# Decay attention followed by an expert layer: the weight conversion of a block split over two steps of the job loop

## The chip, the cores and the metric

The program runs on one core of one Trainium2 chip. Its engines are TensorE (PE in the profile, with its weight loads as PEld), VectorE (DVE), ScalarE (ACT), GpSimd (POOL) and SyncE (SP, which only issues DMAs here). Each engine works through its own list of instructions in order and waits on semaphores for the others. The metric is the device time in microseconds of one execution; lower is better.

## The reference

Decay attention over 8 batches x 8 heads x 576 tokens x 64 dimensions, and then a two-layer expert network on the 4608 tokens, 512 wide inside and out and 2048 wide between:

```python
scores = (q @ k.T) / sqrt(D) + (cum[:, None] - cum[None, :])   # cum = cumsum(log f), causal
attn = softmax(scores);  x = attn @ v                            # heads side by side: 4608 x 512
h = x @ w_in                                                    # 512 x 2048
g = where(h >= 1, h, where(h <= -1, 0, (h + 1) ** 2 / 4))
out = g @ w_out                                                 # 2048 x 512
```

The two weight matrices arrive as 64-bit floats; everything else is 32-bit.

## The kernel before, in words

**Jobs.** Attention is done in jobs, one for a pair of heads of a batch (`jobs`, L80). Batch 0 is cut in two by rows: jobs 0 to 3 take row blocks 0 and 1 (128 rows each) of the four head pairs, jobs 4 to 7 row blocks 2, 3 and 4. From job 8 on, a job has all five row blocks, the last of 64 rows. Jobs 8 to 11 are batch 1, jobs 12 to 15 batch 2, and so on.

**Steps.** A job is a list of steps, one for each row block, with one more step put in for the values product of the job before (`finish`, L796): 3 steps in jobs 1 to 3, 4 in jobs 4 to 7, 6 from job 8 on. A row step (L773) computes the scores of the next row block on PE (L482), builds their decay term on POOL (L488, L492), and for its own row block takes the row minimum on DVE (L571), the exponential on ACT (L575), and writes the result in two half-precision parts, the high one on ACT (L589) and the rest on DVE (L595). These are transposed by a DMA (L601) or, in jobs 0 to 4, by matmuls on PE (`turn_rows`, L513). The last row step of job p also measures the norms of q and k of job p + 2 (`measure`, L391), and the first lines of job p prepare q and k of job p + 1 (`prepare`, L409: L414 on ACT and L416 on DVE write the tile `qs`, and a DMA, L421, transposes it). Jobs below 12 (`NQK`) don't use `qs` for this; job 12 is the first that does.

**Expert units.** A unit is a block of 256 tokens, `ch`, with a block of 256 of the 2048 columns, `fb`. Its front (`moe_front`) is 24 matmuls at L657 into a tile `ph` (48 where the tokens lie in two batches), then ACT and DVE from L666 to L671, which give the two parts of `g`. Its back (`moe_back`) is 12 matmuls at L685 into `po`. Units are handed out by quota after the steps from job 5 on, as their tokens become ready. The order of the first sixteen, written as (ch, fb), is (0,0) to (0,5), (1,0) to (1,5), (0,6), (0,7), (1,6), (1,7). In jobs 9 and 10 these are (1,0), (1,1), (1,2), one each behind steps 1, 3 and 5 of job 9, and (1,3), (1,4), (1,5) behind steps 1, 3 and 5 of job 10; job 11 takes (0,6) and (0,7), behind steps 2 and 5.

**Weight conversion.** There are 16 pieces of weights, numbered n; even ones are from w_in and odd ones from w_out, and pieces 2i and 2i + 1 make block i. `weight_load` (L201) fetches a raw piece of 1 MB to a place given by `RAW`; several pieces use the same place one after the other, so that piece 14 is fetched when piece 12 is done, and piece 15 when piece 14 is done, all three in the place called early. `weight_split` then does, for one block (a single piece for the last two):

- bits and squares: three DVE passes per piece (L211, L214, L217) turn the 64-bit words into 32-bit floats, with the scratch `bits`, which lies in the same memory as `qs`; then ACT squares them and adds them up (L221). The square's own output goes to the low half of `place[n]`, where the converted weights will stand, and that memory can be part of an earlier piece's raw place: that of piece 2 lies in the raw place of piece 0.
- norm product: a matmul of the sums with a matrix of ones on PE (L131), into a tile of the name `ph`, the one that the fronts, `turn_rows` and `across` use also. There are two such buffers.
- scales: four small DVE operations (L132 to L140).
- halves: the high part on ACT (L225), and the low part on POOL for an even piece (L227, L228) or on DVE for an odd one (L230).

`CONVERT` says how many blocks a job converts; they come behind its steps in equal parts, and ahead of the units handed out behind the same step. When the last block of a group of units is done, `moe_scales` computes the scales of that group's units (`early_z`).

**Who sets the order.** A planner at build time orders each engine's list, by the order in which the program traces the instructions and by when it reckons them ready. A few instructions are held by `in_order`: they go behind everything that their engine was given before them. L131 is one of them, and L211 another. In the profile, work of one job is often done while later jobs are running.

Of the kernel before, what the change touches and what calls it, by code (L numbers as in the profile page):

```python
# [45 lines left out]
def kernel(  # L46
# [80 lines left out]
    def from_norms(scale, power, squares):  # L127

        n = squares.shape[1]
        pt = ps.tile([P, 2, TC], F32, name="ph").rearrange("p f t -> p (f t)")  # L130
        in_order(nc.tensor.matmul(pt[:, 0:n], lhsT=ones, rhs=squares, start=True, stop=True))  # L131
        nc.vector.tensor_scalar(  # L132
            out=power, in0=pt[:, 0:n], scalar1=LOW * LOW, scalar2=HIGH * HIGH, op0=ALU.max, op1=ALU.min
        )
        nc.vector.tensor_scalar(
            out=power.bitcast(I32), in0=power.bitcast(I32), scalar1=1, scalar2=EVEN_EXP,
            op0=ALU.logical_shift_right, op1=ALU.bitwise_and,
        )
        nc.vector.tensor_scalar(out=power, in0=power, scalar1=ROOT, scalar2=None, op0=ALU.mult)
        nc.vector.reciprocal(scale, power)  # L140
# [46 lines left out]
    def raw(n):  # L187
        where = RAW[n]
        if where == "early":
            return early.bitcast(I32)[:, 0:4 * DM]  # L190
        if where == "next":
            return x1.bitcast(I32)[:, 0:4 * DM]
        return place[:, where:where + 2].rearrange("p n l c -> p (n l c)").bitcast(I32)
# [6 lines left out]
            src = w_out.bitcast(I32)[i * 2 * P:(i + 1) * 2 * P, :].rearrange("(t p) c -> p t c", p=P)  # L200
        nc.sync.dma_start(raw(n).rearrange("p (t c) -> p t c", t=src.shape[1]), src)  # L201

    def weight_split(n0, n1):
        i, j0 = divmod(n0, 2)
        both = n1 - n0
        m2 = tiny.tile([P, 2], F32, name="m2w", bufs=2)
        words = []
        for n in range(n0, n1):
            top = raw(n)[:, 1::2]
            low = raw(n)[:, 0::2]  # L210
            in_order(nc.vector.tensor_scalar(  # L211
                out=bits, in0=top, scalar1=0x07FFFFFF, scalar2=3, op0=ALU.bitwise_and, op1=ALU.logical_shift_left
            ))
            nc.vector.scalar_tensor_tensor(  # L214
                out=bits, in0=low, scalar=29, in1=bits, op0=ALU.logical_shift_right, op1=ALU.bitwise_or
            )
            nc.vector.scalar_tensor_tensor(  # L217
                out=top, in0=top, scalar=-0x40000000, in1=bits, op0=ALU.bitwise_and, op1=ALU.bitwise_or
            )
            words.append(top.bitcast(F32))  # L220
            nc.scalar.activation(place[:, n, 1], words[-1], AF.Square, accum_out=m2[:, n - n0:n - n0 + 1])  # L221
        from_norms(sw[:, j0:j0 + both, i], mp[:, j0:j0 + both, i], m2[:, 0:both])
        for n, word in zip(range(n0, n1), words):
            hi, lo, s = place[:, n, 0], place[:, n, 1], sw[:, n % 2, i:i + 1]
            nc.scalar.activation(hi, word, AF.Copy, scale=s)  # L225
            if n % 2 == 0:
                nc.gpsimd.tensor_scalar(out=word, in0=word, scalar1=s, scalar2=0.0, op0=ALU.mult, op1=ALU.add)  # L227
                nc.gpsimd.tensor_tensor(out=lo, in0=word, in1=hi, op=ALU.subtract)  # L228
            else:
                nc.vector.scalar_tensor_tensor(  # L230
                    out=lo, in0=word, scalar=s, in1=hi, op0=ALU.mult, op1=ALU.subtract
                )
# [27 lines left out]
    def value_step(b, i):  # L260

        if 0 < i <= NPAIR:
            value_max(b, i - 1)
        if i < NPAIR:
            value_load(b, i)

    def value_scale(b):
        m1 = tiny.tile([P, 1], F32, name="m1", bufs=2)
        nc.vector.tensor_reduce(out=m1, in_=vmax[b], axis=AX.X, op=ALU.max)
        m = mv[:, b:b + 1]  # L270
        across(m, m1)
        if b:
            nc.vector.tensor_tensor(out=m, in0=m, in1=mv[:, b - 1:b], op=ALU.max)
        scale_of(sv[:, b:b + 1], pv[:, b:b + 1], m)
# [84 lines left out]
    def load_decay(w, h):  # L359
        bh = w.b * H + 2 * w.hp + h  # L360
        ck = two.tile([P, S], F32, name="ck", bufs=3)
        nc.sync.dma_start(
            ck[:, 0:w.s1], cum_d[bh:bh + 1, 0:w.s1].broadcast_to([P, w.s1])
        )
        w.ck.append(ck)
# [43 lines left out]
    def prepare(w):  # L409
        if w.p < NQK:  # L410
            return early_prepare(w)
        sc = w.sc
        for j in range(2):
            nc.scalar.activation(qs[:, 2 * j], w.x32[j], AF.Copy, scale=sc[:, j:j + 1])  # L414
        for j in range(2):
            nc.vector.scalar_tensor_tensor(  # L416
                out=qs[:, 2 * j + 1], in0=w.x32[j], scalar=sc[:, j:j + 1], in1=qs[:, 2 * j],
                op0=ALU.mult, op1=ALU.subtract,
            )
        qkT = two.tile([P, 4, SP], F16, name="qkT")  # L420
        nc.sync.dma_start_transpose(  # L421
            qkT.rearrange("p c (b e) -> p (c b) e", e=P), qs.rearrange("p c e -> p (c e)")
        )
        qh, ql, kh, kl = (qkT[:, c] for c in range(4))
        w.terms = ((qh, kh), (ql, kh), (qh, kl))
# [295 lines left out]
    nw = 0  # L721
# [7 lines left out]
    def load_weights(n):  # L729
        nonlocal nload  # L730
        while nload < min(n, 2 * NB) and RAW[nload] not in RAW[nw:nload]:
            weight_load(nload)
            nload += 1

    def weight_step():
        nonlocal nw
        n = nw + (2 if nw < 2 * NB - 2 else 1)
        load_weights(n)
        weight_split(nw, n)
        nw = n  # L740
        load_weights(nw + AHEAD)
        for first, end in groups:
            if nw == 2 * end:
                z = moe_scales(0, first, end - 1, True)
                for ch, e0, e1 in EARLY:
                    if (e0, e1) == (first, end):
                        for fb in range(first, end):
                            bsc[(ch, fb)] = z
# [12 lines left out]
    for p in range(njobs + 1):  # L761
        w = pairs[p] if p < njobs else None
        nxt = pairs[p + 1] if p + 1 < njobs else None
        steps = []
        if w:
            if w.b not in xs:
                xs[w.b] = xpool.tile([P, NPAIR, 2, S], F16, name="x")
            if nxt:
                load_decay(nxt, 0)
                prepare(nxt)  # L770
            scores(w, w.r0)

            def step(r):  # L773
                if r + 1 < w.r1:
                    scores(w, r + 1)
                if r == w.r1 - 2 and nxt:
                    load_decay(nxt, 1)
                    split_values(nxt)
                weights(w, r)
                if r == w.r0 and p + 3 < njobs:  # L780
                    pairs.append(load(p + 3))
                if w.r1 == NT5 and w.b + 1 < B:
                    n = w.r1 - w.r0
                    i = w.hp * n + r - w.r0 - (NPAIR - 1) * n + -(-(NPAIR + 1) // n) * n
                    if 0 <= i <= NPAIR:
                        value_step(w.b + 1, i)
                    if w.hp == NPAIR - 1 and r == w.r0:
                        value_scale(w.b + 1)
                if r == w.r1 - 1 and p + 2 < njobs:
                    measure(pairs[p + 2])  # L790

            steps = [lambda r=r: step(r) for r in range(w.r0, w.r1)]
        if p > 0:
            wp = pairs[p - 1]

            def finish():  # L796
                nonlocal tokens
                (early_values if wp.p < NPE else values)(wp, xs[wp.b])
                if wp.hp == NPAIR - 1:
                    if wp.b and wp.r0 == 0:  # L800
                        join_scales(wp.b - 1)
                    tokens = wp.b * S + wp.s1

            steps.insert(4 if len(steps) == NT5 else 2, finish)
        load_weights(LOADS.get(p, 0))
        blocks = CONVERT.get(p, 0)
        quota = -(-ready() // (NPAIR - (p + NPAIR - 1) % NPAIR))
        before, converted = done, 0
        for i, st in enumerate(steps):
            st()  # L810
            while converted < blocks * (i + 1) // len(steps):
                weight_step()
                converted += 1
            while ready() and done - before < quota * (i + 1) // len(steps):
                if units[done] not in bsc and nw < 2 * NB:
                    break
                moe_unit(*units[done])
                done += 1
# [35 lines left out]
```

## Time and profile before

| what | time or share |
|---|---|
| median of 3 runs | 1116.96 us (1116.5 to 1118.39) |
| the profiled execution | 1118.56 us, its span 1116.8 us |
| mean granted TensorE clock | 0.966 |
| VectorE, ScalarE, GpSimd busy | 799.0, 790.0, 427.4 us |
| DMA | 152.18 MB, mean 136 GB/s |

The profiled execution is one run of its own; what lies outside its span is 1.76 us. In the views that follow, a row of the timeline has the start in microseconds, the busy time, the engine, the line, the operation and its tiles, how often it was merged, and in brackets how long the engine stood idle before it and who ended that wait. A row of the waits has the total, the number and the longest. A row of the windows has, after the stretch and its length, the busy time of PE, PEld, DVE, ACT and POOL with the number of instructions, the granted clock, the share of the DMA engines, and GB/s.

### The profile page before, as it was taken

What the parts mean: (1) busy time and instruction counts of PE and PEld (TensorE: products, weight loads), DVE (VectorE), ACT (ScalarE), POOL (GpSimd) and SP (SyncE); (2) the same over time, 40 slices, a digit from 0 to 9 for tenths busy, and PEclk for the clock granted to TensorE, in tenths of its full rate; (3) what the DMA queues carried; (4) which work ended last, traced back from release to release, by engine and by line L of the source; (5) the groups of instructions that cost most, each with busy time, mean ns of one, the idle gap of its engine ahead of it and who ended that gap; (6) DMA issues with size and microseconds to landing.
All of it is one profiled execution on the core that took longest, in us unless ns stands there. A gap on an engine that the chain in (4) does not pass through costs nothing. (4 is left out here: it accounts for less than half of the span.)

```text
span 1116.8 us, 24410 instructions
## 1 busy us (share of the span) xinstructions
PE 1017.8 (91%) x8811; PEld 663.8 (59%) x8811; DVE 799.0 (72%) x2095; ACT 790.0 (71%) x1638; POOL 427.4 (38%) x679
## 2 busy tenths in 40 slices
PE   4647789667999999999999999999999999999998
PEld 3424455335566666666766666566666666677665
DVE  4785987887989888887667668888888787322222
ACT  3665887756877887788667768787878887444443
POOL 3486665634544543343223324344343442000000
PEclk9968889778999999999999999999999999999999
DMA  7957765575978657766653666775776462200000
GB/s 235 303 143 222 167 147 125 142 191 116 190 172 166 159 143 170 167 152 148 118 140 78 155 119 153 168 174 139 166 167 155 116 124 73 66 21 1 19 20 19
DMA packets 408281, 152.18 MB, mean 136 GB/s; under 512 B 383968, under 2 KB 384992, under 8 KB 408160
## 3 DMA queue, kind: packets, MB, share of 16 engines
q1 hardware_dynamic: 408160, 150.63, 57.6%
q8 instruction: 69, 1.13, 0.4%
q14 instruction: 52, 0.43, 0.1%
HBM read 75.64 MB, written 9.58 MB: 76 GB/s over the span
## 5 line engine op out<-in xcount | busy, mean ns | idle before, releaser
L657 PE MATMUL ph<-x,place 128*128 128x256 f16 (+3 forms) x4608 | 413.3, 248 | 6.4 <-DVE u L668 5.5
L685 PE MATMUL po<-place,g 128*128 128x512 f16 x1728 | 401.9, 382 | 12.4 <-ACT g L670 8.2
L657 PEld LDWEIGHTS <-place 128*128 128x128 f16 x4608 | 354.1, 99 | 66.3 <-issue 18.0
L685 PEld LDWEIGHTS <-g 128*128 128x128 f16 x1728 | 166.4, 99 | 192.0 <-ACT g L670 10.5
L488 POOL TENSOR_SCALAR sdr<-ck,nsig,cqs 128x128 f32<-128x128 f32 (+1 forms) x192 | 145.8, 763 | 149.2 <-DVE pr L595 137.3
L575 ACT ACTIVATE sdr<-sdr,nm 128x384 f32<-128x384 f32 (+1 forms) x248 | 137.4, 554 | 66.9 <-DVE nm L571 57.0
L668 DVE SCALAR_TENSOR_TENSOR u<-ph,z,u 128x512 f32<-128x512 f32 x128 | 95.8, 748 | 113.1 <-ACT u L667 112.5
L488 POOL TENSOR_SCALAR sd<-ck,nsig,cqs 64x576 f32<-64x576 f32 x48 | 60.0, 1250 | 248.7 <-ACT qs L414 109.3
L666 ACT ACTIVATE u<-ph,z 128x512 f32<-128x512 f32 x128 | 97.9, 765 | 78.4 <-PE ph L657 78.4
L482 PE MATMUL s<-qkT 64*64 64x512 f16 (+11 forms) x1056 | 119.6, 342 | 34.1 <-DVE nm L571 30.6
L595 DVE SCALAR_TENSOR_TENSOR pr<-sdr,rc,pr 128x384 f16<-128x384 f32 (+2 forms) x232 | 130.5, 596 | 21.6 <-ACT pr L589 20.4
L670 ACT ACTIVATE g<-u,z 128x512 f16<-128x512 f32 x128 | 91.9, 718 | 67.6 <-DVE u L668 67.3
L671 DVE SCALAR_TENSOR_TENSOR g<-u,z,g 128x512 f16<-128x512 f32 x128 | 96.7, 756 | 47.2 <-ACT g L670 46.5
L589 ACT ACTIVATE pr<-sdr,rc 128x384 f16<-128x384 f32 (+1 forms) x236 | 119.3, 556 | 12.1 <-DVE rc L586 5.3
L571 DVE CUSTOM_DVE_ANT_0 sdr<-s,sdr,nalpha 128x128 f32<-128x128 f32 (+1 forms) x192 | 99.0, 545 | 13.1 <-PE s L482 8.3
L492 POOL TENSOR_SCALAR_AFFINE_SELECT sdr<-sdr 128x128 f32<-128x128 f32 x248 | 93.9, 389 | 9.7
L667 ACT ACTIVATE u<-u 128x512 f32<-128x512 f32 x144 | 89.5, 622 | 2.0
L615 PE MATMUL s<-pT,vs 128*64 128x320 f16 (+3 forms) x1098 | 70.9, 282 | 4.7 <-DVE nm L571 4.7
L615 PEld LDWEIGHTS <-vs 128*64 128x64 f16 x1098 | 49.7, 112 | 27.3 <-issue 8.8
L488 POOL TENSOR_SCALAR sdr<-ck,cq 128x384 f32<-128x384 f32 (+3 forms) x56 | 39.9, 712 | 66.2 <-DVE pr L595 38.3
L482 PEld LDWEIGHTS <-qkT 64*128 64x128 f16 (+1 forms) x864 | 33.8, 99 | 51.3 <-issue 35.9
L414 ACT ACTIVATE qs<-qk,sc 128x640 f16<-128x640 f32 x48 | 37.0, 818 | 22.4 <-DVE sc L140 22.4
(154 smaller groups left out, 1013.8 us busy)
## 6 DMA issues: line engine op xcount, KB each, us to landing
ck<-cum_d SPq DMA_DIRECT2D x64, 288.0 KB, 3.8
out_dram<-ot SPq DMA_DIRECT2D x36, 256.0 KB, 2.1
qk<-in_k_dram SPq DMA_DIRECT2D x64, 128.0 KB, 2.7
vst<-in_v_dram SPq DMA_DIRECT2D x28, 288.0 KB, 3.3
v<-in_v_dram SPq DMA_DIRECT2D x62, 128.0 KB, 2.6
qk<-in_q_dram SPq DMA_DIRECT2D x56, 128.0 KB, 2.7
place<-in_moe_w_in_dram SPq DMA_DIRECT2D x6, 1024.0 KB, 7.2
place<-in_moe_w_out_dram SPq DMA_DIRECT2D x5, 1024.0 KB, 7.2
```

The lines of the kernel that those rows point to most:

```text
L482: nc.tensor.matmul(sds[h % len(sds)][1][p0:p1, c0:c1], lhsT=a[rows, q0 - w.s0:q0 - w.s0 + p1 - p0], rhs=b[rows, c0:c1], start=(i == 0), st ...
L488: nc.gpsimd.tensor_scalar(out=sd[p0:p1, 0:wid], in0=w.ck[h][p0:p1, 0:wid], scalar1=w.nsig if w.p < NQK else w.nsig[p0:p1], scalar2=w.cqs[p ...
L571: nc.vector.tensor_tensor_reduce(out=a, in0=sp[:, 0:wid], in1=a, scale=w.nalpha, scalar=BIG, op0=ALU.add, op1=ALU.min, accum_out=nm[:, i:i ...
L575: nc.scalar.activation(a, a, AF.Exp, bias=nm[:, i:i + 1], scale=-1.0, accum_out=sm[:, i:i + 1])
L589: nc.scalar.activation(pr[:, :, 0, i, :], a, AF.Copy, scale=rc[:, i:i + 1])
L595: nc.vector.scalar_tensor_tensor(out=pr[:, :, 1, i, :], in0=a, scalar=rc[:, i:i + 1], in1=pr[:, :, 0, i, :], op0=ALU.mult, op1=ALU.subtract,)
L615: nc.tensor.matmul(av[64 * h:64 * h + 64, at + s0:at + s1], lhsT=w.vs[:, vl, h, t, :], rhs=w.pT[:, t, pl, h, s0:s1], start=(t == 0 and pi ...
L657: nc.tensor.matmul(ph[:, fi, a0:a1], lhsT=wi[fb][:, wl, t, fi * P:(fi + 1) * P], rhs=xs[b][:, t, xl, s0:s0 + a1 - a0], start=(fi == 0 and ...
L666: nc.scalar.activation(u, h, AF.Relu, scale=z.u[:, i:i + 1], bias=z.h[:, i:i + 1])
L668: nc.vector.scalar_tensor_tensor(out=u, in0=h, scalar=z.t[:, i:i + 1], in1=u, op0=ALU.max, op1=ALU.min)
L671: nc.vector.scalar_tensor_tensor(out=g[:, 1], in0=u, scalar=z.r[:, i:i + 1], in1=g[:, 0], op0=ALU.mult, op1=ALU.subtract)
L685: nc.tensor.matmul(po[ch][i], lhsT=g[:, gl, fi * TC + i * P:fi * TC + (i + 1) * P], rhs=wo[fb][:, wl, fi, :], start=(first and fi == 0 and ...
```

## The change

`weight_split` is cut in two. `weight_words` does the bits and squares of a block, `weight_halves` the norm product, scales and halves. `weight_begin`, at the place where `weight_step` stood, calls the first; `weight_end` calls the second, right behind the following step, ahead of what else stands there. `nw`, the count of pieces done, moves on in `weight_end`, and with it the loads that it allows and the call of `moe_scales`.

```diff
-    def weight_split(n0, n1):
-        i, j0 = divmod(n0, 2)
-        both = n1 - n0
+    def weight_words(n0, n1):
         m2 = tiny.tile([P, 2], F32, name="m2w", bufs=2)
         words = []
         for n in range(n0, n1):
...
             nc.scalar.activation(place[:, n, 1], words[-1], AF.Square, accum_out=m2[:, n - n0:n - n0 + 1])
+        return n0, n1, words, m2
+
+    def weight_halves(n0, n1, words, m2):
+        i, j0 = divmod(n0, 2)
+        both = n1 - n0
         from_norms(sw[:, j0:j0 + both, i], mp[:, j0:j0 + both, i], m2[:, 0:both])
...
-    def weight_step():
-        nonlocal nw
+    half = []
+
+    def weight_begin():
         n = nw + (2 if nw < 2 * NB - 2 else 1)
         load_weights(n)
-        weight_split(nw, n)
-        nw = n
+        half.append(weight_words(nw, n))
+
+    def weight_end():
+        nonlocal nw
+        if not half:
+            return
+        weight_halves(*half[0])
+        nw = half.pop()[1]
         load_weights(nw + AHEAD)
...
             st()
+            weight_end()
             while converted < blocks * (i + 1) // len(steps):
-                weight_step()
+                weight_end()
+                weight_begin()
                 converted += 1
```

By the program's text, with steps counted from 0, this is where the parts stand. The bits and squares stay where they were.

| pieces | bits and squares, and before also the rest | norm product, scales and halves now |
|---|---|---|
| 0, 1 | job 1, step 2 | job 2, step 0 |
| 2, 3 | job 2, step 2 | job 3, step 0 |
| 4, 5 | job 3, step 1 | job 3, step 2 |
| 6, 7 | job 3, step 2 | job 4, step 0 |
| 8, 9 | job 5, step 3 | job 6, step 0 |
| 10, 11 | job 6, step 3 | job 7, step 0 |
| 12, 13 | job 9, step 5 | job 10, step 0 |
| 14 | job 10, step 2 | job 10, step 3 |
| 15 | job 10, step 5 | job 11, step 0 |

The units handed out behind the step of the left column, which stood behind the norm product, now stand ahead of it: (0,1), (0,3), (1,2) and (1,5) among them.

## The prediction

> **What bounds the kernel now.** I read the busy shares first, then PE by stretches, then who PE waited for, and last the order on PE around the norm products.
>
> ```profile
> span 1116.8 us, 24410 instructions
> PE 1017.8 (91%) x8811; PEld 663.8 (59%) x8811; DVE 799.0 (72%) x2095; ACT 790.0 (71%) x1638; POOL 427.4 (38%) x679
> ```
> ```profile
> sum 164.00, PE 120.14 PEld 70.05 DVE 136.22 ACT 115.52 POOL 89.02; mean PE 15.02 PEld 8.76 DVE 17.03 ACT 14.44 POOL 11.13
> 240.00:264.00 24.00, 10.23 (x61) 5.90 (x59) 19.32 (x59) 11.45 (x18) 11.73 (x14) 0.71 0.72 153
> 300.00:400.00 100.00, 99.00 (x977) 65.44 (x977) 84.43 (x228) 80.82 (x172) 43.89 (x72) 1.00 0.75 170
> ```
>
> PE is idle for 99.0 us of the span (1116.8 less 1017.8). The sum row is that of the eight stretches from 100 to 264 us: PE idles 43.9 us there (164.00 less 120.14), 13.8 of it after 240 (24.00 less 10.23). From 300 to 400 it idles 1.0. So the end is set by the amount of matmul work left when PE fills up, at about 264 us. A change of the conversion, which ends there, is worth what it adds to or takes from PE's work before that point, or what it moves that point by.
>
> ```profile
> PE ph L131 <- ACT place L221: 10.9, 4, 5.0
> ```
>
> PE waits four times for squares, 10.9 us in all, because the norm product is pinned to its place on PE. That is what the change can take away at most, if only those waits count. Two of them look free:
>
> ```profile
> 37.19 0.57 ACT L524 ACTIVATE pT<-ph 128x512 f32<-128x512 f32 x1
> 37.34 0.58 PE L131 MATMUL ph<-m2w,ones 128*128 128x2 f32 x2 [1.62 <-ACT place L221]
> 63.83 0.38 PE L131 MATMUL ph<-m2w,ones 128*128 128x2 f32 x2 [1.72 <-ACT place L221]
> 76.46 2.19 PE L482 MATMUL s<-qkT 64*64 64x512 f32 x8 [12.24 <-DVE nm L571]
> ```
>
> Behind the first, PE needs the copy that ends at 37.76 (37.19 + 0.57), and behind the second it stands 12.24 us for VectorE anyway. The other two are 2.58 and 4.97 us:
>
> ```profile
> 181.07 0.83 PE L657 MATMUL ph<-x,place 128*128 128x256 f16 x6
> 205.77 0.58 PE L131 MATMUL ph<-m2w,ones 128*128 128x2 f32 x2 [2.58 <-ACT place L221]
> 206.21 6.89 PE L657 MATMUL ph<-x,place 128*128 128x256 f16 x48
> 233.75 0.38 PE L131 MATMUL ph<-m2w,ones 128*128 128x1 f32 x2
> 234.00 2.78 PE L657 MATMUL ph<-x,place 128*128 128x256 f16 x24
> 247.41 4.15 PE L685 MATMUL po<-place,g 128*128 128x512 f16 x12 [6.87 <-ACT g L670]
> 256.53 0.58 PE L131 MATMUL ph<-m2w,ones 128*128 128x1 f32 x2 [4.97 <-ACT place L221]
> 256.97 4.48 PE L657 MATMUL ph<-x,place 128*128 128x256 f16 x24
> 263.88 1.14 PE L482 MATMUL s<-qkT 64*128 64x128 f16 x12 [1.30 <-DMA qkT<-qs]
> 264.95 3.93 PE L657 MATMUL ph<-x,place 128*128 128x256 f16 x24
> ```
>
> Each of these three products has the next front right behind it, 0.2 to 0.5 us after its start. The 48 matmuls at 206.21 are units (1,2) and (1,3), then come (1,4), (1,5) and, at 264.95, (0,6). No front starts between 181 and 206, though PE has gaps. I take this to be the tile `ph`: product and front share its two buffers, and the planner seems to give them out in the program's order, so that a front traced behind a product can't start ahead of it. The front at 256.97 shows it best, because both buffers had been read long before:
>
> ```profile
> 241.57 0.11 DVE L132 TENSOR_SCALAR pw<-ph 128x2 f32<-128x2 f32 x1
> 245.86 0.74 DVE L668 SCALAR_TENSOR_TENSOR u<-ph,early_z,u 128x512 f32<-128x512 f32 x1
> ```
>
> One was free at 241.7, the other at 246.6, and PE stood idle 6.87 and 4.97 us. So the product doesn't only make PE wait; it holds back expert units that were ready.
>
> **What sets the point at 264 us.** Job 12's scores need `qs`, which is the scratch of the last piece's bits, and that piece's load waits for the halves of piece 14:
>
> ```profile
> 219.80 0.38 SPq L201 DMA_DIRECT2D x<-in_moe_w_in_dram  x1
> 225.43 0.69 DVE L211 TENSOR_SCALAR qs<-x 128x1024 int32<-128x1024 int32 x1 [3.43 <-DMA x<-in_moe_w_in_dram]
> 242.22 2.12 POOL L228 TENSOR_TENSOR place<-x,place 128x1024 f16<-128x1024 f32 x1
> 244.37 0.39 SPq L201 DMA_DIRECT2D x<-in_moe_w_out_dram  x1
> 250.96 1.17 DVE L211 TENSOR_SCALAR qs<-x 128x1024 int32<-128x1024 int32 x1 [1.48 <-DMA x<-in_moe_w_out_dram]
> 255.27 1.11 ACT L221 ACTIVATE place<-x 128x1024 f16<-128x1024 f32 x1 [6.71 <-DVE x L217]
> 259.35 2.70 SPq L421 DMA_TRANSPOSE qkT<-qs  x1
> ```
>
> Load of piece 14 at 219.80, its bits from 225.43, its halves done at 244.34, load of piece 15 at 244.37, its bits from 250.96, its square, `qs`, the transpose at 259.35, PE at 263.88. This chain passes through the products of pieces 12/13 and 14, not through that of 15.
>
> **The change part by part.** No instruction is added or removed; parts of nine conversions are traced a step later, and with them the loads that `nw` allows, on SP's queue. The two rows of L211 above are its only waits for a load, so of the loads only those of pieces 14 and 15 have no slack.
>
> *Piece 15.* Its product moves behind unit (1,5). The front of (1,5), 4.48 us at the clock of that stretch, then fits in the idle 6.87 us ahead of 247.41; its work on ACT and DVE falls where ACT stood 6.71 us; and its back can fill most of the 4.97 us ahead of 256.53. At 256.97 the next front, (0,6), takes the place that (1,5) had. So one front and one back more are done before 264. Late in the kernel, where PE is full, they cost (from the chain of work that ended last):
>
> ```profile
> 1024.49 2.62 PE ph L657 x24
> 1027.11 2.59 PE po L685 x12
> ```
>
> That is 2.62 + 2.59 = 5.2 us off the end. If (0,7) too runs before 264, in the second buffer, it is 7.8; if the planner leaves the order as it is, 0. I take 5.2.
>
> *Pieces 12/13.* Unit (1,2) can run before 205.77. It fills a gap, but the stretch up to 264 is held by the chain above, so nothing comes of it by itself: bounds 0 and 2.6, the wait. I take 0. The same holds of (0,1) and (0,3) and their products in jobs 6 and 7, whose ACT and DVE work also moves; 0 here, and a rival below.
>
> *Does the chain get longer?* The products at 205.77 and 233.75 are traced a step later, but the planner already runs them about a job late: job 11's first row minimum is at 219.49, its last at 240.72.
>
> ```profile
> 219.49 0.28 DVE L571 CUSTOM_DVE_ANT_0 sdr<-s,sdr 128x128 f32<-128x128 f32 x1
> 240.72 0.75 DVE L571 CUSTOM_DVE_ANT_0 sd<-s,sd 128x576 f32<-128x576 f32 x1
> ```
>
> The product of piece 14, now of job 10's step 3, runs at 233.75 amid job 11's rows. What it is pinned behind on PE has been issued, and what competes with its halves on DVE, ACT and POOL is still traced later. So I take 0; the bounds are 0 and two steps, one for each halves in the chain, of 5.3 us each ((240.72 - 219.49) / 4).
>
> *Pieces 0 to 7.* In the short jobs a step later is later in fact. The first product goes behind the matmuls of job 2's first row, from 37.34 to about 49.
>
> ```profile
> 47.68 1.22 PE L513 MATMUL ph<-pr,sdr 128*128 128x128 f32 x4
> 48.52 1.14 ACT L221 ACTIVATE place<-place 128x1024 f16<-128x1024 f32 x1 [0.60 <-issue]
> 42.85 2.11 POOL L228 TENSOR_TENSOR place<-place 128x1024 f16<-128x1024 f32 x1
> ```
>
> The halves of piece 0 ended 7.6 us after the product (42.85 + 2.11 - 37.34), so now at about 56.5 (48.9 + 7.6). The square of piece 2, at 48.52, writes into piece 0's raw place and must wait for that: up to 8 us for it, and for whatever the planner leaves behind it on ACT. Against that, POOL and DVE are freed of halves around 41 to 45, when they hold up job 2. Bounds: 8.0 us lost, and 2.1 won, the POOL pass taken out; I take 0, nearest to the two free waits above, since PE stands idle from 64 to 76 in any case.
>
> A price that moves about unseen is that of POOL's pass beside DVE:
>
> ```profile
> 242.14 0.16 DVE L297 TENSOR_SCALAR z<-z 128x8 f32<-128x8 f32 x1
> 242.28 2.09 DVE L298 TENSOR_SCALAR z<-z 128x8 f32<-128x8 f32 x1
> ```
>
> A tiny operation took 2.09 us beside L228 in place of 0.16. One such meeting more or less on the chain is 1.9 us either way. The Trainium skill ("SBUF — State Buffer", section "SBUF: two separate sides") says that the pair of ports shared by VectorE and GpSimd is an exclusive lock, where the loser "fully blocks". The row agrees. By that rule the eight POOL passes block DVE before and after alike, and only where they fall changes; a halves that falls on job rows speaks against the change, by those 1.9 us.
>
> **The sum.** 1118.56 us for the profiled execution, less 5.2, is 1113.4. That execution lies 1.6 us above the median of the runs shown, so the forecast on the median is 1116.96 - 5.2 = 1111.8 us.
>
> **The rivals.** *The units win more.* If the three earlier units, each a front of 2.62 us, also shorten jobs 6 to 11, 7.9 us come on top: 1103.9. For it speak the 43.9 us of idle PE from 100 to 264; against it, that VectorE is busy 136.22 of those 164 us, and that the chain of loads sets the pace.
>
> *Nothing changes.* The planner orders by readiness, and if it has the squares ready early, product and front keep their order: 1117.0. The back-to-back pairs above speak against it.
>
> *The conversion chain gets longer: slower.* The halves of pieces 12 and 14 come a step late in fact, load 14 and load 15 with them, and VectorE, whose bits are pinned, waits for them at L211 as it already does (3.43 and 1.48 us). Job 12 then starts up to 10.6 us later, less the 5.2 won: 1122.4; one step only gives 1117.1. It decides from 5.2 us of delay on, 7.4 for a loss that can be seen. The dependence of squares on older halves in jobs 2 and 3 works the same way. For it: every link of the chain hangs on halves, and the change delays only those.
>
> **How the numbers follow.** About 0.2% (2.2 us) is what a measurement of this kernel can tell from no change. Forecast, 2.3 to 8 us won (1109.0 to 1114.7): 0.45. More: 0.12. Within 2.2 us, which holds "nothing changes" and a loss that eats the gain: 0.18. Slower: 0.25. So faster 0.57, same 0.18, slower 0.25. The range goes from 1104.5, near the end of the larger gain, to 1121.0, short of the two full steps.
>
> **What would show it.** Right: no wait of L131 for L221 near 205 and 256; a front between 241 and 247; (0,6) or its like before job 12's scores; those scores still near 264; PE idle from 240 to 264 about 5 us less. Wrong: L211 waiting longer for its DMA, job 12's scores after 269, or an ACT wait for POOL's L228 near 50.

## The result, and the profile after

The changed kernel is slower: 1131.21 us median (1130.64 to 1133.31, four runs), against 1117.68 us (1116.5 to 1118.69, four runs) for the kernel before beside it. The ratio is 1.0125, with a 95% interval from 1.0107 to 1.0143, some 13.5 us. The forecast was 1111.8 us, and its range ended at 1121.0. The profiled execution took 1131.65 us; its page begins:

```profile
span 1129.8 us, 24406 instructions
PE 1029.5 (91%) x8811; PEld 667.7 (59%) x8811; DVE 800.0 (71%) x2095; ACT 790.0 (70%) x1638; POOL 421.3 (37%) x679
```

The span is 13.0 us longer, and PE is busy 11.7 us longer with the same 8811 matmuls. (Lines from 209 on have moved: the bits are now L209 to L215, the square L219, the high half L228, the low half L230 and L231 on POOL and L233 on DVE, `turn_rows` L516, the front L660, the back L688.)

The windows view, cut where the prediction cut it and once more at 300 us, shows where the loss stands. First the kernel before, then the changed one:

```profile
0.00:264.00 264.00, 178.22 (x1074) 108.73 (x1076) 199.84 (x518) 174.70 (x375) 147.89 (x211) 0.86 0.72 184
264.00:300.00 36.00, 33.37 (x292) 21.14 (x291) 31.84 (x108) 29.88 (x69) 19.86 (x29) 0.95 0.73 144
300.00:1116.80 816.80, 806.25 (x7449) 533.88 (x7448) 567.28 (x1470) 585.42 (x1196) 259.65 (x440) 1.00 0.53 120
```
```profile
0.00:264.00 264.00, 184.48 (x1066) 111.48 (x1066) 191.62 (x492) 171.20 (x370) 143.14 (x208) 0.88 0.69 178
264.00:300.00 36.00, 27.51 (x206) 15.10 (x205) 32.48 (x110) 26.25 (x57) 15.27 (x24) 0.87 0.61 139
300.00:1129.80 829.80, 817.53 (x7543) 541.08 (x7541) 575.95 (x1495) 592.51 (x1214) 262.90 (x448) 1.00 0.54 121
```

Up to 300 us PE is busy equally long (178.22 + 33.37 = 211.6 and 184.48 + 27.51 = 212.0 us), but it has done less: 1366 matmul records before, 1272 after. So 817.53 us of work is left in place of 806.25, 11.3 us more, and PE idles 1.7 us more behind 300 (12.3 for 10.6). Together these are the 13.0. Idle time up to 300 us says nothing of the loss; the matmuls done do.

Most of the signs of being right that the prediction named for the stretch from 200 to 270 us appear. From the waits, and then from the timeline of the changed kernel (SP's loads and PE):

```profile
PE ph L131 <- ACT place L219: 8.7, 4, 3.5
```
```profile
217.79 0.38 PE L131 MATMUL ph<-m2w,ones 128*128 128x2 f32 x2 [1.24 <-ACT place L219]
...
227.26 0.38 SPq L201 DMA_DIRECT2D x<-in_moe_w_in_dram  x1
...
252.52 2.67 PE L660 MATMUL ph<-x,place 128*128 128x256 f16 x23 [1.50 <-DVE pw L132]
...
254.62 0.38 SPq L201 DMA_DIRECT2D x<-in_moe_w_out_dram  x1
...
268.42 0.38 PE L131 MATMUL ph<-m2w,ones 128*128 128x1 f32 x2 [0.51 <-ACT place L219]
268.67 1.58 PE L660 MATMUL ph<-x,place 128*128 128x256 f16 x13
...
276.26 1.14 PE L485 MATMUL s<-qkT 64*128 64x128 f16 x12 [4.82 <-DMA qkT<-qs]
```

The last product waits 0.51 us for its square (4.97 before), that of pieces 12 and 13 1.24 (2.58); unit (1,5), at 252.52, runs ahead of the last product, and (0,6), at 268.67, ahead of job 12's scores. But all of it stands later: load 14 by 7.5 us, load 15 by 10.3, job 12's scores by 12.4, which puts them past the 269 us that the prediction named as a sign of being wrong. So the chain was late before its first link. The delay starts in job 3, at 60 to 105 us. The timeline of VectorE before, bits of piece 6, low halves of pieces 3 and 5, last row minimum of job 5:

```profile
62.58 1.55 DVE L211 TENSOR_SCALAR qs<-place 128x1024 int32<-128x1024 int32 x1
64.05 1.75 DVE L230 SCALAR_TENSOR_TENSOR place<-place,sw 128x1024 f16<-128x1024 f32 x1
...
78.49 1.27 DVE L230 SCALAR_TENSOR_TENSOR place<-place,sw 128x1024 f16<-128x1024 f32 x1
...
95.42 0.75 DVE L571 CUSTOM_DVE_ANT_0 sd<-s,sd 128x576 f32<-128x576 f32 x1
```

And the changed kernel, VectorE with GpSimd and TensorE:

```profile
75.59 2.12 POOL L231 TENSOR_TENSOR place<-place 128x1024 f16<-128x1024 f32 x1
75.67 2.07 DVE L135 TENSOR_SCALAR mp<-mp 128x2 int32<-128x2 int32 x1
...
80.82 1.29 DVE L233 SCALAR_TENSOR_TENSOR place<-place,sw 128x1024 f16<-128x1024 f32 x1 [2.43 <-ACT place L228]
82.03 2.60 DVE L209 TENSOR_SCALAR qs<-place 128x1024 int32<-128x1024 int32 x1
...
94.19 0.59 PE L131 MATMUL ph<-m2w,ones 128*128 128x2 f32 x2 [3.43 <-ACT place L219]
94.64 3.76 PE L516 MATMUL ph<-pr,sdr 128*128 128x128 f32 x16
...
95.01 0.17 DVE L135 TENSOR_SCALAR mp<-mp 128x2 int32<-128x2 int32 x1
...
96.94 1.20 POOL L230 TENSOR_SCALAR place<-place,sw 128x1024 f32<-128x1024 f32 x1 [9.26 <-ACT place L228]
...
104.19 0.75 DVE L574 CUSTOM_DVE_ANT_0 sd<-s,sd 128x576 f32<-128x576 f32 x1
```

The bits of piece 6 now start at 82.03, right behind the low half of piece 5, 19.5 us later than before. Everything behind them follows: the norm product of pieces 6 and 7 at 94.19 (81.91 before), the row transposes behind it on PE, GpSimd idle for 9.26 us with the low half of piece 6 at the head of its list and ScalarE's high half not ready, and job 5's last minimum 8.8 us late.

The kernel before shows what `in_order` is not: there the bits of piece 6, at 62.58, run ahead of the low halves of pieces 3 and 5, which were traced before them. It doesn't hold an instruction behind everything that its engine was given earlier, as the text ahead of the prediction has it. What fits is one edge (this instruction not before that one), to the instruction that the engine was given directly before. The experiments below test it. Before the change that was an instruction of step 2 of job 3. After it, `weight_end` (pieces 4 and 5) and `weight_begin` (pieces 6 and 7) stand side by side in that step, and the instruction directly ahead of the bits is the low half of piece 5, the very last of that block's conversion.

### The profile page after: what moved, and what is told of

It reads as the page before. It is cut to its first block, busy times and chain, and to the rows that moved or that the text cites. A ratio compares the mean times of both kernels' runs of the same rounds, so it can differ in the third digit from the quotient of the medians.

```text
span 1129.8 us, 24406 instructions
## 1 busy us (share of the span) xinstructions
PE 1029.5 (91%) x8811; PEld 667.7 (59%) x8811; DVE 800.0 (71%) x2095; ACT 790.0 (70%) x1638; POOL 421.3 (37%) x679
## 5 line engine op out<-in xcount | busy, mean ns | idle before, releaser
L660 PE MATMUL ph<-x,place 128*128 128x256 f16 (+3 forms) x4608 | 414.4, 249 | 8.0 <-DVE u L671 5.4
L688 PE MATMUL po<-place,g 128*128 128x512 f16 x1728 | 403.1, 383 | 6.7 <-DVE g L674 3.1
L660 PEld LDWEIGHTS <-place 128*128 128x128 f16 x4608 | 354.8, 99 | 67.2 <-issue 19.4
L688 PEld LDWEIGHTS <-g 128*128 128x128 f16 x1728 | 166.3, 99 | 186.4 <-issue 7.7
L491 POOL TENSOR_SCALAR sdr<-ck,nsig,cqs 128x128 f32<-128x128 f32 (+1 forms) x192 | 142.3, 745 | 145.3 <-DVE pr L598 120.0
L598 DVE SCALAR_TENSOR_TENSOR pr<-sdr,rc,pr 128x384 f16<-128x384 f32 (+2 forms) x232 | 134.4, 613 | 20.3 <-ACT pr L592 18.8
L485 PE MATMUL s<-qkT 64*64 64x512 f16 (+11 forms) x1056 | 125.7, 354 | 24.4 <-DVE nm L574 11.4
L618 PEld LDWEIGHTS <-vs 128*64 128x64 f16 x1098 | 49.6, 111 | 27.5 <-issue 10.3
```

What stands on the lines that cost most here:

```text
L485: nc.tensor.matmul(sds[h % len(sds)][1][p0:p1, c0:c1], lhsT=a[rows, q0 - w.s0:q0 - w.s0 + p1 - p0], rhs=b[rows, c0:c1], start=(i == 0), st ...
L491: nc.gpsimd.tensor_scalar(out=sd[p0:p1, 0:wid], in0=w.ck[h][p0:p1, 0:wid], scalar1=w.nsig if w.p < NQK else w.nsig[p0:p1], scalar2=w.cqs[p ...
L598: nc.vector.scalar_tensor_tensor(out=pr[:, :, 1, i, :], in0=a, scalar=rc[:, i:i + 1], in1=pr[:, :, 0, i, :], op0=ALU.mult, op1=ALU.subtract,)
L618: nc.tensor.matmul(av[64 * h:64 * h + 64, at + s0:at + s1], lhsT=w.vs[:, vl, h, t, :], rhs=w.pT[:, t, pl, h, s0:s1], start=(t == 0 and pi ...
L660: nc.tensor.matmul(ph[:, fi, a0:a1], lhsT=wi[fb][:, wl, t, fi * P:(fi + 1) * P], rhs=xs[b][:, t, xl, s0:s0 + a1 - a0], start=(fi == 0 and ...
L688: nc.tensor.matmul(po[ch][i], lhsT=g[:, gl, fi * TC + i * P:fi * TC + (i + 1) * P], rhs=wo[fb][:, wl, fi, :], start=(first and fi == 0 and ...
```

## The experiments

The theory: the loss is made by that one edge in job 3, and the rest of the change is worth little. The rivals: the chain of loads 14 and 15 lengthens by itself (the prediction's own slower rival); several late blocks add up; the order of the text does it without the edge. The medians of the kernel before differ from chip to chip, so the ratio counts; it is an estimate from all the runs and not the quotient of the two medians. Under 0.2% it isn't told from no change.

| kernel | median us | before, same chip | ratio, 95% interval |
|---|---|---|---|
| split in jobs 1 to 3 | 1133.67 | 1118.04 | 1.0148 (1.0123 to 1.0172) |
| split in jobs 5 and 6 | 1121.02 | 1118.04 | 1.0032 (1.0011 to 1.0052) |
| split in jobs 9 and 10 | 1115.92 | 1118.04 | 0.9984 (0.9969 to 1.0) |
| changed, bits 6 and 7 first | 1116.32 | 1118.04 | 0.9995 (0.998 to 1.0009) |
| split of 4 and 5 only | 1123.64 | 1119.02 | 1.0038 (1.0023 to 1.0054) |
| split of all but 4 and 5 | 1117.29 | 1119.02 | 0.9986 (0.997 to 1.0001) |
| bits first, but behind the scales | 1124.57 | 1119.02 | 1.0047 (1.003 to 1.0064) |
| bits first, jobs 5 and 6 whole | 1115.84 | 1119.02 | 0.9975 (0.9961 to 0.9988) |
| changed, bits 6 and 7 not held | 1117.88 | 1118.69 | 0.999 (0.9976 to 1.0004) |
| changed, low half of 6 on VectorE | 1122.86 | 1118.69 | 1.0045 (1.0027 to 1.0063) |
| before, low half of 6 on VectorE | 1115.53 | 1118.69 | 0.9962 (0.9943 to 0.9981) |
| split of piece 15 only | 1119.56 | 1118.69 | 1.0005 (0.999 to 1.0021) |
| changed, halves of 6 and 7 later still | 1125.86 | 1117.38 | 1.0076 (1.0061 to 1.0092) |
| bits first, 5 and 6 whole, low half of 6 on VectorE | 1115.17 | 1117.38 | 0.9986 (0.9975 to 0.9997) |
| split in 9 and 10, low half of 6 on VectorE | 1113.78 | 1117.38 | 0.997 (0.9959 to 0.998) |

### Which jobs lose

The three runs share one edit, with (1, 2, 3), (5, 6) and (9, 10) for `SPLIT`:

```diff
+SPLIT = (1, 2, 3)
...
                 weight_end()
                 weight_begin()
+                if p not in SPLIT:
+                    weight_end()
                 converted += 1
```

> The split is kept in jobs 1 to 3 alone (pieces 0 to 7); in jobs 5, 6, 9 and 10 a block's product, scales and halves follow its squares at once, as before. Kernel before 1117.7 us, changed kernel 1131.2. Theory (the loss is made early and handed on: in the changed kernel the last row minimum of job 7 is already 5.7 us late, of job 11 15.0): about half of the loss appears, 1124 us. Rival (the pieces 12, 14 and 15 lengthen the chain of their own loads by themselves): 1118, since those pieces are as before.

> The split is kept in jobs 5 and 6 alone (pieces 8 to 11). Theory (the square of piece 10 waits 5.73 us for POOL's late halves of piece 8, and ACT's queue behind it): 1122 to 1124 us, some 5 us of the 13.5. Rival (only pieces 12, 14 and 15 lose): 1118.

> The split is kept in jobs 9 and 10 alone (pieces 12 to 15). Theory (the loss is made in jobs 3, 5 and 6): the unit (1,5) moved ahead of the last product is worth what was forecast, and the time is 1112 to 1114 us. Rival (each of the two late halves in the chain of loads costs a step): 1128 to 1131, most of the loss.

The early jobs alone lose 1.48%, as much as the whole change (the intervals overlap); the theory had put only half of it there. Jobs 5 and 6 lose 0.32%, less than the 5 us expected. Jobs 9 and 10 alone, the part on which the forecast was built, win 0.16%, hardly told from none, where the theory had 4 to 6 us and the rival a loss. In that run load 14 stands at 215.56 and job 12's scores at 263.82 (219.80 and 263.88 before): its own late halves don't move the end of the chain, though the chain takes 4.2 us longer from load 14 on. The three parts don't add up exactly (1.48 + 0.32 - 0.16 is 1.64, the whole is 1.25). What the 0.32% of jobs 5 and 6 are made of was not taken further.

### The order in job 3

Only the order within step 2 of job 3 is turned round; the split and all else stay:

```diff
     def weight_begin():
-        n = nw + (2 if nw < 2 * NB - 2 else 1)
+        n0 = half[-1][1] if half else nw
+        n = n0 + (2 if n0 < 2 * NB - 2 else 1)
...
-        nw = half.pop()[1]
+        nw = half.pop(0)[1]
...
-            weight_end()
+            if p != 3 or i == 0:
+                weight_end()
             while converted < blocks * (i + 1) // len(steps):
-                weight_end()
-                weight_begin()
+                if p == 3:
+                    weight_begin()
+                    if len(half) > 1:
+                        weight_end()
+                else:
+                    weight_end()
+                    weight_begin()
```

> The changed kernel, but in step 2 of job 3 the bits and squares of pieces 6 and 7 are traced ahead of the norm product, scales and halves of pieces 4 and 5, so that the bits, held in order on VectorE, are not behind that block's low half. Theory (that order puts the bits of piece 6 from 62.6 to 82.0 us, and job 5 and the loads of pieces 10 and 12 with them): 5 us less than the changed kernel, 1126. Rival (the early blocks have slack, the loss is later): 1131, as the changed kernel.

The whole loss goes, not 5 us of it: 0.9995. The bits of piece 6 start at 68.57 and job 5's last minimum at 98.04. This says where the loss is made, but not yet that the held edge makes it. Two runs narrow it to a block: the same `if` around a `weight_end()` as above, with `if nw != 4` and with `if nw == 4` for its condition, so that the split is kept for pieces 4 and 5 alone, and for all the others:

```diff
                 weight_begin()
+                if nw != 4:
+                    weight_end()
```

> The split is kept for the block of pieces 4 and 5 alone; every other block is converted at once, as before. Theory (the loss is that block's halves, traced directly ahead of the bits of piece 6, which VectorE keeps in order behind them): the bits of piece 6 stand near 82 us and most of the loss is there, 1129 to 1133 us, with 15 of 16 pieces untouched. Rival (several late blocks together, as pieces 0 to 3, whose halves the squares of 2 and 3 wait for): under 1122.

> The changed kernel, but the block of pieces 4 and 5 is converted at once in step 1 of job 3, as before. Theory (that one block): 1116 to 1119 us, no loss left. Rival (late blocks together): 1125 or more.

Without the split of 4 and 5 nothing is lost (0.9986). With that split alone 0.38% is lost, far from the expected 1129 or more. The timeline of that run:

```profile
71.28 1.61 DVE L233 SCALAR_TENSOR_TENSOR place<-place,sw 128x1024 f16<-128x1024 f32 x1 [3.00 <-ACT place L228]
72.82 0.68 DVE L209 TENSOR_SCALAR qs<-place 128x1024 int32<-128x1024 int32 x1
```

The edge is there, the bits of piece 6 right behind the low half of piece 5, but that low half ends at 72.89 and not at 82.11. With pieces 0 to 3 converted at once, the bits of piece 4 start at 55.30; in the changed kernel they start at 60.29. So the loss has two parts that need each other: the split of pieces 0 to 3 makes block 4 and 5 late, which by itself is harmless, and the edge hands this on to piece 6. Where the 0.38% of the edge alone is lost isn't shown: job 5's last minimum stands at 97.77 in that run, as late as in the run without the hold below (97.77), which loses nothing.

Which instruction holds the bits was tried by putting the product and the scales of pieces 4 and 5, but not their halves, back ahead of the bits (`weight_norms` is the call of `from_norms` taken out of `weight_halves`, which for this block leaves it out):

```diff
...
-        from_norms(sw[:, j0:j0 + both, i], mp[:, j0:j0 + both, i], m2[:, 0:both])
+        if n0 != 4:
+            weight_norms(n0, n1, m2)
...
             if p != 3 or i == 0:
                 weight_end()
+            elif i == 2:
+                weight_norms(half[0][0], half[0][1], half[0][3])
```

> The kernel that traced the bits of pieces 6 and 7 first, but with the norm product and the scales of pieces 4 and 5 put back ahead of them; only the halves stay behind. It tells which part of the block holds the bits. Theory (the halves: VectorE's low half of piece 5 waits for ScalarE's high half and ends at 82.1 us in the changed kernel): bits of piece 6 near 72, 1116 to 1119 us. Rival (the scales: they wait for the squares and the product, 75.5 to 78.1 us): bits of piece 6 near 78 and 1124 or more.

```profile
77.90 0.17 DVE L140 RECIPROCAL sw<-mp 128x2 f32<-128x2 f32 x1
77.98 0.67 DVE L209 TENSOR_SCALAR qs<-place 128x1024 int32<-128x1024 int32 x1
...
101.96 0.75 DVE L580 CUSTOM_DVE_ANT_0 sd<-s,sd 128x576 f32<-128x576 f32 x1
```

The rival was right: the bits start at 77.98, and 0.47% is lost. The reciprocal at 77.90 is now the instruction traced directly ahead of the bits, and they start behind its end. It need not be a costly instruction: this one takes 0.17 us, but it is the last of four small operations behind a product on another engine. (The last row minimum is L580 in this kernel.)

Last, the edge itself. The text, the split and the place of all halves stay as changed; only the bits of pieces 6 and 7 are no longer held:

```diff
-            in_order(nc.vector.tensor_scalar(
+            (in_order if n not in (6, 7) else lambda op: op)(nc.vector.tensor_scalar(
                 out=bits, in0=top, scalar1=0x07FFFFFF, scalar2=3, op0=ALU.bitwise_and, op1=ALU.logical_shift_left
             ))
```

> The changed kernel with one thing less: the first pass of the bits of pieces 6 and 7 is no longer held in order behind what VectorE was given before it. The program's text, the split and the place of every halves stay as changed. Theory (that hold is what turns a halves traced earlier into a delay of the next bits): the bits of piece 6 are back near 69 us and the time is 1116 to 1118 us, all of the loss gone. Rival (the order of the text itself, through the planner's priorities): 1125 or more.

```profile
68.27 0.68 DVE L209 TENSOR_SCALAR qs<-place 128x1024 int32<-128x1024 int32 x1
...
74.63 0.74 DVE L209 TENSOR_SCALAR qs<-x 128x1024 int32<-128x1024 int32 x1
...
97.77 0.76 DVE L574 CUSTOM_DVE_ANT_0 sd<-s,sd 128x576 f32<-128x576 f32 x1
```

The ratio is 0.999, and the loss is gone with two edges less. The text is unchanged, so the cause is the held edge, not the order of the text.

Over all the runs the start of the bits of piece 6 tells who loses. It lies at 61.8 to 69.1 us in every run that lost nothing, and at 72.8 to 82.8 in those that lost, but for the split in jobs 5 and 6 (62.40), which touches other blocks.

### What carries the delay on

Two carriers were suspected between the late bits and job 5: GpSimd's queue, where the low half of piece 6 stands ahead of decay terms, and the norm product on TensorE. The first was tried by moving that low half to VectorE, in the changed kernel and in the kernel before:

```diff
-            if n % 2 == 0:
+            if n % 2 == 0 and n != 6:
                 nc.gpsimd.tensor_scalar(out=word, in0=word, scalar1=s, scalar2=0.0, op0=ALU.mult, op1=ALU.add)
                 nc.gpsimd.tensor_tensor(out=lo, in0=word, in1=hi, op=ALU.subtract)
```

> The changed kernel with the low half of piece 6 in one pass on VectorE instead of two on GpSimd. The bits of piece 6 stay near 82 us. Theory (what carries the delay on is GpSimd's queue: the low half of piece 6 stands ahead of job 5's decay terms and holds them for 9.26 us): job 5's last row minimum comes 5 to 8 us earlier than 104.19 and the time is 1120 to 1124 us. Rival (the delay is carried by the norm product on TensorE at 94.19 or by the loads of pieces 10 and 12 at 100 and 102 us, which stay): 1129 or more.

> The kernel before with the same edit, the low half of piece 6 on VectorE: what that edit is worth by itself, to be taken off the run beside it. All theories: near the kernel before, 1116 to 1120 us (GpSimd is free of some 4 us at 85 to 89, VectorE has 1.3 us more to do).

The edit alone is worth 0.38%, which no theory had foreseen. In the changed kernel it takes the loss from 1.25 to 0.45%, that is 0.8, of which 0.4 is the edit's own. In the kernel before with this edit, job 5's decay terms start at 86.13 us in place of 89.20 and its last minimum comes at 93.26 in place of 95.42, which fits the gain. But in the changed kernel job 5's last minimum moves by only 2.2 us, and its timeline says why:

```profile
94.54 0.59 PE L131 MATMUL ph<-m2w,ones 128*128 128x2 f32 x2 [3.44 <-ACT place L219]
94.99 3.76 PE L516 MATMUL ph<-pr,sdr 128*128 128x128 f32 x16
...
98.43 2.33 POOL L491 TENSOR_SCALAR sdr<-ck,cq 128x512 f32<-128x512 f32 x2 [10.40 <-PE ph L516]
...
101.97 0.75 DVE L574 CUSTOM_DVE_ANT_0 sd<-s,sd 128x576 f32<-128x576 f32 x1
```

GpSimd, freed of the low half, now waits 10.40 us for the row transposes, which read the tiles that it is to write, and these stand on TensorE behind the product. So the product was tried: the conversion's end for pieces 6 and 7 is traced one step later still, which leaves the bits late and makes the halves later yet, but puts the product behind those transposes.

```diff
             st()
-            weight_end()
+            if p != 4 or i >= 1:
+                weight_end()
```

> The changed kernel, but the norm product, scales and halves of pieces 6 and 7 are traced one step later still, behind step 1 of job 4 in place of step 0. The bits of piece 6 stay held near 82 us, and the weights themselves are ready later. Theory (the product on TensorE, with GpSimd's low half behind it, stands ahead of job rows and holds them): TensorE runs the 16 row transposes near 88 to 90 in place of 94.64, job 5's last row minimum comes at 95 to 98 in place of 104.19, and the time falls to 1118 to 1124 us although the halves come later. Rival (late weights: units, loads and later conversions wait for them): 1131 or more.

```profile
82.75 2.62 DVE L209 TENSOR_SCALAR qs<-place 128x1024 int32<-128x1024 int32 x1
83.09 1.16 PE L516 MATMUL ph<-pr,sdr 128*128 128x128 f32 x8 [1.01 <-ACT pT L527]
...
85.24 1.16 PE L516 MATMUL ph<-pr,sdr 128*128 128x128 f32 x8
...
92.28 0.75 DVE L574 CUSTOM_DVE_ANT_0 sd<-s,sd 128x576 f32<-128x576 f32 x1
...
98.28 0.59 PE L131 MATMUL ph<-m2w,ones 128*128 128x2 f32 x2 [7.80 <-ACT place L219]
```

The transposes are done by 86.4, job 5's last minimum comes at 92.28, 11.9 us earlier than in the changed kernel, and the time falls by half a per cent (1.0076 for 1.0125) although the weights are ready later. The low half on GpSimd moves with the product here; but taking away that low half alone won job 5 only 2.2 us, so the product ahead of the transposes is a carrier. It isn't the only one: 0.76% is still lost with job 5 on time, a little above the theory's end of 1124. That the rest is the late weights themselves fits the rival, but no run shows it.

### What the moved unit is worth

```diff
                 weight_begin()
+                if nw != 15:
+                    weight_end()
```

> The split is kept for piece 15 alone. The prediction put 5.2 us of gain on it: the front and back of unit (1,5) done ahead of its product. With pieces 12 to 15 split the gain was only 2. Theory (the unit is worth 5 and the split of pieces 12 to 14 takes 3 back): 1113 to 1114 us against 1118 to 1119 before. Rival (moving the unit ahead is itself worth only about 2, since (0,6) no longer runs in the gap that (1,5) left): 1116 to 1117.

Neither: 1.0005, with an interval that allows from 1.1 us won to 2.3 lost. The unit does move. On TensorE in this run, unit (1,5) runs at 240.70 ahead of the last product, and (0,6) at 258.91 (with a VectorE pass of unit (1,5) and job 12's first scores):

```profile
240.70 2.78 PE L660 MATMUL ph<-x,place 128*128 128x256 f16 x24 [1.19 <-DVE pw L132]
...
252.40 0.73 DVE L674 SCALAR_TENSOR_TENSOR g<-u,early_z,g 128x512 f16<-128x512 f32 x1
...
258.66 0.38 PE L131 MATMUL ph<-m2w,ones 128*128 128x1 f32 x2 [3.57 <-ACT place L219]
258.91 4.45 PE L660 MATMUL ph<-x,place 128*128 128x256 f16 x24
...
265.76 0.67 PE L485 MATMUL s<-qkT 64*128 64x128 f16 x12 [2.41 <-DMA qkT<-qs]
```

The windows of the fronts' line alone (busy time and, in brackets, matmuls), first before, then in this run:

```profile
0.00:264.00 264.00, 39.55 (x288) 0.86 0.72 184
264.00:280.00 16.00, 9.49 (x72) 0.90 0.44 96
280.00:300.00 20.00, 5.62 (x72) 1.00 0.97 182
```
```profile
0.00:264.00 264.00, 41.98 (x312) 0.88 0.70 184
264.00:280.00 16.00, 6.79 (x48) 0.79 0.55 117
280.00:300.00 20.00, 5.73 (x74) 1.00 0.88 177
```

One front (24 matmuls) more by 264 us, as forecast; none more by 280 (360 and 360), and two matmuls by 300 (432 and 434). The lead is given back right behind 264. Job 12's scores start at 265.76 there, 1.9 us later than before (263.88), although load 15 was issued 1.0 us earlier (243.38), and from 264 to 280 TensorE is busy 13.40 us (16.00 before) at a granted clock of 0.79 (0.90). On VectorE a pass of unit (1,5), at 252.40, now stands between the bits passes of piece 15, and the last of these starts at 256.15 (254.01 before). That these passes are what makes the scores late fits the rows, but no run parts it.

### A version that beats both

The part that won and the edit that won were put together, with pieces 6 and 7 first or with the early jobs whole:

```diff
                     weight_end()
                     weight_begin()
+                    if p in (5, 6):
+                        weight_end()
```

> The kernel that traced the bits of pieces 6 and 7 first, and in jobs 5 and 6 the blocks are converted at once, as before. Theory (the split of jobs 5 and 6 alone cost 3 us against the kernel before): 3 us less than with it, 1113 us. Rival (with job 3 mended, jobs 5 and 6 run earlier and the split there costs nothing): 1116.

> The kernel with the bits of pieces 6 and 7 first and jobs 5 and 6 converted at once (1115.8 us), with the low half of piece 6 on VectorE (worth 3.2 us in the kernel before). Theory (the two gains are apart: one is TensorE's order around 240 to 264 us, the other GpSimd's queue around 86): 1112 to 1113.5 us. Rival (the low half already lies beside other work there): 1115 to 1116.

> The kernel before with the split in jobs 9 and 10 alone and the low half of piece 6 on VectorE. Theory (gains of 2.1 and 3.2 us add): 1113 us. Rival (the second gain is given back before 300 us, as that of piece 15 alone was): 1115 to 1116.

The first diff, put upon the kernel with the bits first, beats the kernel before by 0.25%. The median is that of the rival, not the 1113 of the theory; but the kernel before was slower on this chip, and by the ratios (0.9995 and 0.9975, with overlapping intervals) the step is 0.2%, between the two. Neither is decided. With the low half of piece 6 on VectorE as well the gain is not larger (0.14%, the two intervals overlap). The split in jobs 9 and 10 with that low half wins 0.30%, 1113.78 us, but the low half by itself won 0.38%. So no gain is seen to add to another; for this last pair, where the sum would be 0.54%, the intervals don't rule it out. All of them end some 2 to 4 us under the kernel before.

## Why the prediction was wrong

- **The step that failed** is "Pieces 0 to 7", taken at 0 "nearest to the two free waits above, since PE stands idle from 64 to 76 in any case". Jobs 1 to 3 cost 1.48% (1.23 to 1.72), 14 to 19 us. The step priced a wait on ScalarE and looked at TensorE for cover. Its priced wait came true and was small: the square of piece 2 moved from 48.52 to 56.57, by the 8 us of the bound, and cost ScalarE 1.75 us of waiting. With GpSimd's passes over piece 0, which now stand ahead of the decay terms of job 3 (the last of these at 56.49 in place of 52.84), it goes with the bits of piece 4 starting at 60.29 in place of 55.11. That alone lost nothing (the split of all but 4 and 5). What turned it into a loss was on VectorE, where the step looked only at pieces 0 to 2: which instruction stands directly ahead of a block's first held pass once the halves have moved. For eight of the nine blocks that is no instruction of a conversion; for pieces 6 and 7 it is.

```profile
56.57 1.13 ACT L219 ACTIVATE place<-place 128x1024 f16<-128x1024 f32 x1 [1.75 <-POOL place L231]
```

- **"Piece 15: 5.2 us"** was right in its mechanism and mis-sized. Product and front share the tile `ph`, the product did hold the unit, and the unit did move. It measured 0.05% lost, with 0 well inside the interval. The premise under it was wrong: a front more by 264 us isn't a front less at the end, because TensorE isn't bound by its own work alone from 264 on. The step found room for the unit's work where ScalarE stood idle, and put nothing on its passes on VectorE, which runs the bits of piece 15 for job 12; job 12's scores came 1.9 us later and the lead was gone by 280.
- **"What sets the point at 264"**, the chain of loads 14 and 15, was right as a description: every link moved, and job 12's scores with them. It was an effect here, not the cause.
- **"Does the chain get longer": 0** was right in its end for the halves of pieces 12 and 14 themselves. Jobs 9 and 10 alone bring load 14 forward by 4.2 us and leave the scores where they were.
- **Pieces 12 and 13: 0** was not tried alone; all of jobs 9 and 10 won 0.16%, hardly told from none, so nothing speaks against it. The fronts of jobs 6 and 7, also put at 0, were off by the 0.32% of jobs 5 and 6, if that is theirs.
- **The slower rival** had the sign, a size of 5.4 us (1122.4 less 1117.0) for 13.5, and the wrong place. Its sentence that the dependence in jobs 2 and 3 "works the same way" named nearly the right jobs, but through squares that wait for older halves.
- **POOL's pass beside DVE, 1.9 us**: the rows at 75.67 and 95.01 show it, the first on the path that counted. The same tiny operation took 0.17 us with GpSimd idle and 2.07 beside L231, ahead of the bits of piece 6, whose own first pass then took 2.60 beside the next L231 (81.12 to 84.09 us), in place of 0.68 in the run without the hold. The rule of the Trainium skill ("SBUF — State Buffer", section "SBUF: two separate sides"), that the two engines can lock each other out of a shared pair of ports, agrees with these rows; it gives no order, and the order made the loss.
- **The signs.** Those of being right that came, at 200 to 270 us, are local: they say that a wait went, not when the stretch begins. Of the three signs of being wrong two came: job 12's scores at 276.26, after the 269 named, and ScalarE waiting for POOL's pass, 1.75 us at 56.57. The third, a longer wait of the bits for their loads, did not (0.28 us and none, for 3.43 and 1.48). No sign looked at the bits of piece 6 on VectorE.

## What to carry to other kernels

When a traced part of a program moves, list for every held instruction what now stands directly ahead of it on its engine, and when that is done; a cheap instruction at the end of a chain across engines holds as hard as a costly one. Work pulled into an idle gap is a gain only if nothing else paces what comes behind the gap: count the matmuls done at several later points, before and after, and see whether the lead is still there. Try the parts of a change one by one, since here one loss hid three parts that were each worth nothing or a little.

## What the hardware showed besides

The same work can cost TensorE more in a thinly filled stretch than in a full one. The same 24 matmuls of a front took 2.78 us at 240.70 and 4.45 at 258.91 in the run with piece 15 alone. In a window of the changed kernel and then one of the kernel before, each cut closely around one front, the granted clock (the third number from the end) is 0.60 for a front of 4.61 us and 1.00 for one of 2.78:

```profile
242.60:247.40 4.80, 4.69 (x26) 3.23 (x25) 2.37 (x7) 1.31 (x5) 2.58 (x6) 0.60 0.50 124
```
```profile
234.00:236.80 2.80, 2.80 (x28) 2.33 (x29) 2.62 (x8) 2.80 (x8) 2.46 (x6) 1.00 0.49 120
```

In the 10 us ahead of the slow front TensorE was busy 5.87 us, ahead of the fast one 8.19; in the run with piece 15 alone the same count gives 5.07 ahead of the slow front and 8.81 ahead of the fast one. The Trainium skill ("TensorE: Matmul & The Clock Gate", section "Part 1: The HAM clock gate (the 'warmup' mystery)") says that the clock is gated by how busy the array has been lately; these rows agree in direction. That it explains the equal busy time and the 94 matmul records less up to 300 us isn't shown: the mean granted clock up to there is 0.88 in the changed kernel and 0.87 in the kernel before.

Not foreseen either: the low half of one piece, done in one pass on VectorE, which is the busier engine, in place of two on GpSimd, made the kernel 0.38% faster (0.19 to 0.57).
